# Attention and token-mixing kernel on one core: the last third of x transposed by the DMA, attention in half groups, eager first scores, last store in pieces

## The chip, the cores and the metric

The kernel runs on one core of a Trainium2 chip. The metric is device time in microseconds (us) of one execution. Times below are medians of the fast executions of a kernel; executions of one kernel here lie within 0.2 to 1.4% of each other (kernel before: 223.94 to 224.87). A ratio is the mean time of one kernel's fast runs over that of the other's in the same rounds, so it isn't quite the ratio of the medians that are quoted. A profile covers the span from the first to the last instruction of one execution, some 2 us less than its time; what is counted in a trace is counted in that execution alone.

TensorE is the matrix engine, VectorE and ScalarE the two elementwise engines, GpSimd casts inputs here, and SyncE issues nearly all DMAs. In the profile they are PE, DVE, ACT, POOL and SP; PEld is the weight load of TensorE.

## The reference, cut to what matters

```python
# 8 batches, 16 query heads, 4 key/value heads, 384 positions, head size 64
scores = (1/sqrt(64)) * q @ k.T            # per head
attn   = exp(scores - max) / sum
x      = attn @ v                          # -> 8 x 384 x 1024
wq, wk = x @ w_q, x @ w_k                  # 1024 -> 64
W_tok  = (1/sqrt(64)) * wq @ wk.T          # 384 x 384 per batch
out    = relu(W_tok @ x) @ w_out           # 1024 x 1024
```

The product `x @ [w_q w_k]` needs x with its 1024 features on the partitions, so each batch's x (three thirds of 128 positions) has to be transposed. In the kernel this product is `wqk`; it needs all three thirds, and everything after it for that batch (`wk_tr`, `mix_c`, `mix_m`, `po`) needs its result.

## The kernel before

The order of instructions isn't written out; a small scheduler inside the kernel keeps a clock for TensorE (`clk["pe"]`), estimates when each operand will be there (`ready`), and always emits the best candidate. Each engine gets its list in that order; how strictly TensorE keeps to it shows below, where it stands idle for 4.37 us in front of one instruction with others behind it in the list. The estimates are guesses made when the kernel is built.

```python
    def x_tr_dma(b, c):                                   # third c of batch b, by the DMA
        ...
        nc.sync.dma_start_transpose(out=xTs[b][:, :, c, :], in_=xn[:, c, :])
        ready["T", b, c] = when(("X", b, c, 0), ("X", b, c, 1)) + 4500     # the guess: 4.5 us

    def x_tr(b, c):                                       # the same by TensorE and VectorE
        ...
        for dc in range(DC):
            nc.tensor.transpose(out=ps[:, dc, :], in_=xn[:, c, dc * P:(dc + 1) * P], identity=ident)
        nc.vector.tensor_copy(out=xTs[b][:, :, c, :], in_=ps)

    def attend(b, g):                                     # one group: two halves, a PSUM bank each
        ...
        if b > 0 and c < C - 1 and kp == KP - 1:
            x_tr_dma(b, c)                                # thirds 0 and 1 of batches 1 to 7

    def wqk(b):                                           # needs xT of all three thirds
        ...
        for dc in range(DC):
            nc.tensor.matmul(out=ps, lhsT=wqk_sb[:, dc, :],
                             rhs=xT[:, dc].rearrange("d c p -> d (c p)"),
                             start=(dc == 0), stop=(dc == DC - 1))

    def after_s(b, s):                                    # SyncE's work, tied to the score steps
        n = b + 1
        ...
        if s == 0:
            load(n)                                       # 2.36 MB: keys, queries in two halves, values
        elif s == 5:
            cast(n)                                       # GpSimd, to bf16
            start_tr(n)
        elif s in (9, 11, 13, 15):
            tr_dma(n, (s - 9) // 2)                       # keys, then queries in thirds, transposed by the DMA
```

The loads, the transposes and the stores all go out on SyncE's one queue, in the order in which the scheduler emits them.

The softmax here doesn't subtract the row's maximum and nothing guards it: scores larger than these inputs give would overflow.

## Time and profile before

| | kernel before |
|---|---|
| time, median | 223.95 us (first three runs), 224.35 with a fourth |
| TensorE busy | 92% of 221.7 us |
| ScalarE, VectorE busy | 64%, 65% |
| DMA engines busy | over 90% in most slices up to 160 us |
| waits of TensorE after 45 us | none worth counting |

The prediction below shows the lines. Three more are needed for the comparison: the granted clock of TensorE in 40 slices (9 is 90% or more), the chain of work that ended last, and the group of `wqk` (its columns: line, engine, operation, operands, count, busy us and mean ns, then the idle time just before and what ended it).

```profile
PEclk9999999999999999999999999999999999999999
...
PE 87%; ACT 4%; DVE 4%; issue 2%; DMA 1%; ACTq 0%
...
L328 PE MATMUL bank<-xT,wqk_sb 128*128 128x384 bf16 x64 | 11.8, 327 | 0.0
```

The clock has no dent, the chain is TensorE nearly throughout, and `wqk` never waited: 0.0 us of idle time before its 64 matmuls.

### The profile page before, as it was taken

Reading aid. Unit: us, or ns where it says so; the run is one execution under the profiler, and the core shown is the slowest. Engines: PE = TensorE matmul, PEld = TensorE weight load, DVE = VectorE, ACT = ScalarE, POOL = GpSimd, SP = SyncE. Lnnn points to the kernel's source line nnn. Section 1 sums busy time; section 2 is a strip of 40 time slices with the busy share of each in tenths; the row PEclk is TensorE's granted clock in tenths of the full one; section 3 lists DMA queues with packets and bytes.
Section 4 is the critical chain, followed back from the end, with each engine's and each line's share of the span. In section 5 each row is a group of like instructions: output and inputs, shape, how many; then the busy total and the mean of one; then the engine's idle time right before and its main releaser. Section 6 shows DMA issues by size and latency. Waiting matters only on the chain.

```text
span 221.7 us, 5331 instructions
## 1 busy us (share of the span) xinstructions
PE 204.7 (92%) x2164; PEld 106.5 (48%) x2164; DVE 144.1 (65%) x363; ACT 140.9 (64%) x146; POOL 52.3 (24%) x97
## 2 busy tenths in 40 slices
PE   1686899799999999999999999999999998999992
PEld 0264575446454645454546454644554553434440
DVE  2363776946786678768866687665876578475341
ACT  3588988978877887788788868787778730000000
POOL 1378757304400440027004400260000000000000
PEclk9999999999999999999999999999999999999999
DMA  6999999899869978899999997998422420332433
GB/s 166 329 326 263 418 368 290 159 232 353 132 186 237 348 98 220 196 324 242 154 272 348 147 223 194 336 209 163 142 95 52 142 95 3 146 138 95 191 143 143
DMA packets 71400, 46.09 MB, mean 208 GB/s; under 512 B 42704, under 2 KB 67280, under 8 KB 71376
## 3 DMA queue, kind: packets, MB, share of 16 engines
q1 hardware_dynamic: 71376, 45.75, 78.0%
q8 instruction: 17, 0.28, 0.5%
q14 instruction: 7, 0.06, 0.1%
HBM read 23.59 MB, written 12.58 MB: 163 GB/s over the span
## 4 chain that ended last, share of the span: by engine, by line
PE 87%; ACT 4%; DVE 4%; issue 2%; DMA 1%; ACTq 0%
PE bank L405 39%; PE bank L277 16%; PE sc L247 16%; PE bank L328 5%; ACT pt L251 4%; PE bank L359 3%; PE bank L381 2%; PE bank L319 2%; PE bank L212 2%; DMA kraw<-in_k_dram 1%; DVE xnat L286 1%; DVE wT L334 1%; DVE wq L336 0%; PE bank L346 0%; PE bank L196 0%
## 5 line engine op out<-in xcount | busy, mean ns | idle before, releaser
L251 ACT ACTIVATE pt<-sc 128x1024 bf16<-128x1024 f32 x144 | 139.2, 1021 | 34.9 <-PE sc L247 34.8
L405 PE MATMUL bank<-wout_sb,msb 128*128 128x512 bf16 x384 | 94.6, 380 | 0.3 <-DVE msb L386 0.3
L405 PEld LDWEIGHTS <-msb 128*128 128x128 bf16 x384 | 33.9, 97 | 45.9 <-issue 14.5
L247 PE MATMUL sc<-QT,KT 64*128 64x512 bf16 x288 | 46.2, 389 | 5.1 <-ACT pt L251 3.9
L277 PEld LDWEIGHTS <-pt 128*128 128x128 bf16 x1152 | 41.3, 98 | 14.0 <-issue 4.6
L414 DVE COPY osb<-bank 128x512 f32<-128x512 f32 x48 | 33.0, 688 | 21.8 <-PE bank L405 21.6
L277 PE MATMUL bank<-vext,pt 128*128 128x65 bf16 x1152 | 45.4, 194 | 1.4 <-ACT pt L251 1.4
L286 DVE TENSOR_TENSOR xnat<-bank,rcp 128x256 bf16<-128x256 f32 x96 | 40.8, 425 | 3.3
L386 DVE TENSOR_SCALAR msb<-bank 128x384 bf16<-128x384 f32 x64 | 32.3, 550 | 3.9 <-PE bank L381 3.7
L146 POOL CAST qb<-qraw 128x768 bf16<-128x768 f32 x30 | 24.0, 829 | 19.4 <-DMA qraw<-in_q_dram 15.7
L285 DVE RECIPROCAL rcp<-bank 128x4 f32<-128x4 f32 x96 | 17.0, 177 | 17.5 <-PE bank L277 17.1
L247 PEld LDWEIGHTS <-KT 64*128 64x128 bf16 x288 | 12.9, 94 | 25.8 <-issue 21.8
L141 POOL CAST kb<-kraw 128x192 bf16<-128x192 f32 x30 | 9.2, 350 | 65.9 <-DMA kraw<-in_k_dram 65.9
L328 PE MATMUL bank<-xT,wqk_sb 128*128 128x384 bf16 x64 | 11.8, 327 | 0.0
L381 PE MATMUL bank<-wq,Csb 64*128 64x384 bf16 x32 | 10.4, 326 | 0.1
L381 PE MATMUL bank<-wT,Csb 64*128 64x384 bf16 x32 | 10.4, 326 | 0.0
L363 DVE CAST Csb<-bank 128x512 bf16<-128x512 f32 x8 | 5.5, 692 | 7.5 <-PE bank L359 7.5
L334 DVE CAST wT<-bank 128x384 bf16<-128x384 f32 x8 | 4.5, 558 | 7.7 <-PE bank L328 7.7
L320 DVE COPY xT<-bank 128x1024 bf16<-128x1024 bf16 x10 | 6.7, 688 | 3.6 <-PE bank L319 3.6
L586 POOL CAST wout_sb<-wld 128x1024 bf16<-128x1024 f32 x8 | 8.1, 1042 | 3.9 <-DMA wld<-in_moe_w_out_dram 3.9
L328 PEld LDWEIGHTS <-wqk_sb 128*128 128x128 bf16 x64 | 5.7, 98 | 5.6 <-issue 1.9
L154 POOL CAST vext<-vraw 128x384 bf16<-128x384 f32 x16 | 7.8, 510 | 0.0
(30 smaller groups left out, 55.2 us busy)
## 6 DMA issues: line engine op xcount, KB each, us to landing
out_dram<-osb SPq DMA_DIRECT2D x24, 512.0 KB, 2.8
qraw<-in_q_dram SPq DMA_DIRECT2D x15, 768.0 KB, 8.7
wld<-in_moe_w_out_dram SPq DMA_DIRECT2D x4, 1024.0 KB, 8.2
kraw<-in_k_dram SPq DMA_DIRECT2D x7, 384.0 KB, 4.3
vraw<-in_v_dram SPq DMA_DIRECT2D x7, 384.0 KB, 9.2
qraw<-in_q_dram SPq DMA_DIRECT2D x1, 512.0 KB, 6.0
kraw<-in_k_dram SPq DMA_DIRECT2D x2, 192.0 KB, 4.2
vraw<-in_v_dram SPq DMA_DIRECT2D x2, 192.0 KB, 6.8
```

The costliest lines, as they stand in the source:

```text
L141: eng.tensor_copy(out=nats[b][0][:, kp, :, u, :], in_=raws[b][0][:, 2 * kp + u])
L146: eng.tensor_copy(out=nats[b][1][:, :, kp, :, u, :].rearrange("p c i d -> p i c d"), in_=raws[b][2][:, h0:h0 + G])
L247: nc.tensor.matmul(out=ps[:, u, :], lhsT=KT[lo:hi, kp * C + kc, :], rhs=QT[lo:hi, t0:t0 + G, :].rearrange("k i p -> k (i p)"), start=True, ...
L251: nc.scalar.activation(out=pt.rearrange("k u i p -> k u (i p)"), in_=ps, func=AF.Exp, scale=attn_scale)
L277: nc.tensor.matmul(out=outs[u][:, i * DE:i * DE + D + 1], lhsT=tiles[kc][:, u, i, :], rhs=vext[:, 2 * kp + u, kc, :D + 1], start=(kc == 0) ...
L285: nc.vector.reciprocal(out=rcp, in_=avv[:, :, D])
L286: nc.vector.tensor_tensor(out=xout[:, u], in0=avv[:, :, :D], in1=rcp.to_broadcast([P, G, D]), op=ALU.mult)
L328: nc.tensor.matmul(out=ps, lhsT=wqk_sb[:, dc, :], rhs=xT[:, dc].rearrange("d c p -> d (c p)"), start=(dc == 0), stop=(dc == DC - 1))
L381: nc.tensor.matmul(out=bank_ps[i][:, :S], lhsT=Csb[lo:hi, j * P:(j + 1) * P], rhs=w[lo:hi, :], start=True, stop=True)
L386: nc.vector.tensor_scalar_max(out=msb[:, dc, :], in0=bank_ps[i][:, :S], scalar1=0.0)
L405: nc.tensor.matmul(out=ps, lhsT=msbs[b][:, dc, c * P:(c + 1) * P], rhs=wout_sb[:, dc, half * NH:(half + 1) * NH], start=(nd == 0), stop=(n ...
L414: nc.vector.tensor_copy(out=osb[:, half * NH:(half + 1) * NH], in_=ps)
```

## The change

Its intent: take 48 transposes off TensorE, the engine that sets the time; let attention start when one PSUM bank is free rather than two; feed ScalarE without gaps in batch 0; hold the column-tiled product (`mix_c`) back when a score burst is near; and let the last store start earlier. Cut to its core:

```diff
+    EAGER = 0
+    DMA_TR = 5500
@@ guesses of the scheduler for a DMA transpose
-                ready["K", b, kp] = clk["pe"] + 4500
+                ready["K", b, kp] = clk["pe"] + DMA_TR
@@ attend: one half u per call, one bank
-    def attend(b, g):
+    def attend(b, g, u):
 ...
-        if b > 0 and c < C - 1 and kp == KP - 1:
+        if x_by_dma(b, c) and kp == KP - 1:
             x_tr_dma(b, c)
+
+    def x_by_dma(b, c):
+        return b > 0 and (c < C - 1 or b < B - 1)
@@ po: the last store
+            if last:
+                (nc.sync if n0 % NH == 0 else nc.scalar).dma_start(out=dst[:, n0:n1], in_=osb[:, n0:n1])
@@ chain_open
-            if b == 0 or c == C - 1:
+            if not x_by_dma(b, c):
                 todo.append((..., lambda c=c: x_tr(b, c), 1))
-        todo.append((lambda: when(("N", b)), lambda: mix_c(b), 1))
+        todo.append((lambda: when(("N", b)), lambda: mix_c(b), 1, "tiled"))
@@ step
-            row = todo[0][2] == 2
-            if row and pair is not None and pair < now + 1200:
+            if todo[0][-1] == "tiled" and pair is not None and pair < now + 1200:
                 prio = 6
-            cands.append((s0 + 30, 7, go_s))
+            cands.append((s0, 0, go_s) if state["S"][0] <= EAGER else (s0 + 30, 7, go_s))
```

More of the change, by code (lines that the diff above doesn't have):

```diff
@@ L185, in tr_dma @@
             for kp in range(KP):
-                ready["Q", b, kp, c] = clk["pe"] + 4500
+                ready["Q", b, kp, c] = clk["pe"] + DMA_TR
     def tr_k(b, kp0, kp1):
@@ L253, in scores @@
         pts[b, s] = pt
-        done = on("act", 1020, pe(225, "row"))
+        done = on("act", 1020, pe(225 if b else 430, "row"))
         clk["act"] = done - 60 - 100
@@ L257, in scores @@
         ready["P", b, s] = done
-    def attend(b, g):
+    def attend(b, g, u):
         kp, c = groups(b)[g]
         vext = vexts[b % 3]
-        if g == 0:
+        if g == 0 and u == 0:
             xnats[b] = x_p.tile([P, C, Hq, D], BF16, name="xnat", bufs=3)
-        xnat = xnats[b]
-        tiles = [pts.pop((b, C * g + kc)) for kc in range(C)]
-        h0 = 2 * kp * G
-        xout = xnat[:, c, h0:h0 + 2 * G, :].rearrange("p (u i) d -> p u i d", u=2)
-        if NWIDE:
-            _, at = wide()
-            outs = [wide_ps[at][:, u, :] for u in range(2)]
-        else:
-            two = [bank(u)[1] for u in range(2)]
-            outs = [bank_ps[i] for i in two]
-        for u in range(2):
-            for i in range(G):
-                for kc in range(C):
-                    nc.tensor.matmul(out=outs[u][:, i * DE:i * DE + D + 1],
-                                     lhsT=tiles[kc][:, u, i, :],
-                                     rhs=vext[:, 2 * kp + u, kc, :D + 1],
-                                     start=(kc == 0), stop=(kc == C - 1))
-            if NWIDE:
-                continue
-            avv = outs[u][:, :G * DE].rearrange("p (i e) -> p i e", i=G)
-            rcp = small_p.tile([P, G], F32, name="rcp", bufs=4)
-            nc.vector.reciprocal(out=rcp, in_=avv[:, :, D])
-            nc.vector.tensor_tensor(out=xout[:, u], in0=avv[:, :, :D],
-                                    in1=rcp.to_broadcast([P, G, D]), op=ALU.mult)
-            done = bank_free[two[u]] = on("dve", 665, pe(370))
-        if NWIDE:
-            avv = wide_ps[at][:, :, :G * DE].rearrange("p u (i e) -> p u i e", i=G)
-            rcp = small_p.tile([P, 2, G], F32, name="rcp")
-            nc.vector.reciprocal(out=rcp, in_=avv[:, :, :, D])
-            nc.vector.tensor_tensor(out=xout, in0=avv[:, :, :, :D],
-                                    in1=rcp.to_broadcast([P, 2, G, D]), op=ALU.mult)
-            done = wide_free[at] = on("dve", 935, pe(750))
-        ready["X", b, c, kp] = done
-        if b > 0 and c < C - 1 and kp == KP - 1:
@@ new lines, in attend @@
+        tiles = [pts[b, C * g + kc] for kc in range(C)]
+        at = bank()[1]
+        ps = bank_ps[at]
+        for i in range(G):
+            for kc in range(C):
+                nc.tensor.matmul(out=ps[:, i * DE:i * DE + D + 1], lhsT=tiles[kc][:, u, i, :],
+                                 rhs=vext[:, 2 * kp + u, kc, :D + 1],
+                                 start=(kc == 0), stop=(kc == C - 1))
+        avv = ps[:, :G * DE].rearrange("p (i e) -> p i e", i=G)
+        rcp = small_p.tile([P, G], F32, name="rcp", bufs=4)
@@ new lines, in attend @@
+        nc.vector.reciprocal(out=rcp, in_=avv[:, :, D])
+        h0 = (2 * kp + u) * G
+        nc.vector.tensor_tensor(out=xnats[b][:, c, h0:h0 + G, :], in0=avv[:, :, :D],
+                                in1=rcp.to_broadcast([P, G, D]), op=ALU.mult)
+        bank_free[at] = on("dve", 665, pe(370 if b else 630))
+        if u == 0:
+            return
+        for kc in range(C):
+            pts.pop((b, C * g + kc))
+        ready["X", b, c, kp] = bank_free[at]
+        if x_by_dma(b, c) and kp == KP - 1:
@@ L310, in x_tr_dma @@
         nc.sync.dma_start_transpose(out=xTs[b][:, :, c, :], in_=xn[:, c, :])
-        ready["T", b, c] = when(("X", b, c, 0), ("X", b, c, 1)) + 4500
+        ready["T", b, c] = when(("X", b, c, 0), ("X", b, c, 1)) + DMA_TR
     def x_tr(b, c):
@@ L413, in po @@
         osb = osbs[b, c]
-        nc.vector.tensor_copy(out=osb[:, half * NH:(half + 1) * NH], in_=ps)
+        dst = out[b].rearrange("(p c) n -> c p n", c=C)[c]
+        last = b == B - 1 and c == C - 1
+        for n0 in range(half * NH, (half + 1) * NH, NH // 2 if last and half else NH):
+            n1 = n0 + (NH // 2 if last and half else NH)
+            nc.vector.tensor_copy(out=osb[:, n0:n1], in_=ps[:, n0 - half * NH:n1 - half * NH])
+            if last:
+                (nc.sync if n0 % NH == 0 else nc.scalar).dma_start(out=dst[:, n0:n1], in_=osb[:, n0:n1])
         bank_free[i] = on("dve", 690, end)
-        if half == 1:
-            nc.sync.dma_start(out=out[b].rearrange("(p c) n -> c p n", c=C)[c], in_=osb)
-    state = {"S": (0, 0), "A": (0, 0)}
+        if half == 1 and not last:
+            nc.sync.dma_start(out=dst, in_=osb)
+    state = {"S": (0, 0), "A": (0, 0, 0)}
     prep = []
@@ L454, in cand_a @@
     def cand_a():
-        b, g = state["A"]
+        b, g, u = state["A"]
         if b == B:
             return None
-        return max(when(*[("P", b, C * g + kc) for kc in range(C)]), ready["V", b],
-                   wide()[0] if NWIDE else bank(1)[0])
+        return max(when(*[("P", b, C * g + kc) for kc in range(C)]), ready["V", b], bank()[0])
     def go_a():
-        b, g = state["A"]
-        attend(b, g)
-        if g + 1 == C * KP:
+        b, g, u = state["A"]
+        attend(b, g, u)
+        if u == 0:
+            state["A"] = (b, g, 1)
+        elif g + 1 == C * KP:
             chain_open(b)
-            state["A"] = (b + 1, 0)
+            state["A"] = (b + 1, 0, 0)
         else:
-            state["A"] = (b, g + 1)
+            state["A"] = (b, g + 1, 0)
     def chain_open(b):
@@ L476, in chain_open @@
         todo.append((lambda: when(("W", b)), lambda: wk_tr(b), 1))
-        todo.append((lambda: when(("N", b)), lambda: mix_c(b), 1))
+        todo.append((lambda: when(("N", b)), lambda: mix_c(b), 1, "tiled"))
         for j in range(DC // 2):
-            todo.append((lambda: when(("C", b), ("W2", b)), lambda j=j: mix_m(b, j), 2))
+            todo.append((lambda: when(("C", b), ("W2", b)), lambda j=j: mix_m(b, j), 2, "tiled"))
         chains[b] = todo
@@ L484, in cand_chain @@
     def cand_chain(b):
-        at, _, width = chains[b][0]
-        if chains.get(b - 2) or (width == 2 and any(job[0] <= b - 2 for job in bulk)):
+        at, _, width = chains[b][0][:3]
+        if chains.get(b - 2) or (len(chains[b]) == DC // 2 and any(job[0] <= b - 2 for job in bulk)):
             return INF
@@ L542, in step @@
                 todo = chains[b]
-                if todo and todo[0][2] == 2 and cand_chain(b) <= clk["pe"] + 20:
+                if todo and todo[0][-1] == "tiled" and cand_chain(b) <= clk["pe"] + 20:
                     todo.pop(0)[1]()
@@ L604 @@
         pass
-    assert state["A"] == (B, 0) and not bulk and not prep
+    assert state["A"] == (B, 0, 0) and not bulk and not prep
 _INS = ['q', 'k', 'v', 'moe_w_q', 'moe_w_k', 'moe_w_out']
```

## The prediction

> **What bounds the kernel now.** I read the page's busy shares and slices first, then the groups, then the waits of TensorE, and last the timeline of the SyncE queue with the landing times of single DMAs.
>
> ```profile
> PE 204.7 (92%) x2164; PEld 106.5 (48%) x2164; DVE 144.1 (65%) x363; ACT 140.9 (64%) x146; POOL 52.3 (24%) x97
> ...
> PE   1686899799999999999999999999999998999992
> ...
> DMA  6999999899869978899999997998422420332433
> ```
>
> TensorE is full from slice 8 (some 45 us) to slice 39; before that it waits for inputs and for ScalarE's exponentials. What is easily missed is the last line: the DMA engines are nearly as full as TensorE, up to about 160 us.
>
> ```profile
> PE sc L247 <- ACT pt L251: 3.9, 6, 1.0
> PE bank L277 <- ACT pt L251: 1.4, 4, 0.4
> PE sc L247 <- DVE QT L222: 1.0, 2, 0.5
> ```
>
> These are the longest of TensorE's waits after the one for the first keys (4.2 us), and every one falls in the first 44 us. So in the middle the time is the sum of what TensorE is given, and any new wait of TensorE there is paid in full, since nothing is idle that could be used up later.
>
> ```profile
> 71.83 0.62 PE L319 MATMUL bank<-ident,xnat 128*128 128x128 bf16 x8
> 72.29 0.81 PE L405 MATMUL bank<-wout_sb,msb 128*128 128x512 bf16 x3
> 72.94 0.91 PE L277 MATMUL bank<-vext,pt 128*128 128x65 bf16 x24
> 73.78 0.61 PE L247 MATMUL sc<-QT,KT 64*128 64x512 bf16 x4
> 74.31 1.47 PE L328 MATMUL bank<-xT,wqk_sb 128*128 128x384 bf16 x8
> ```
>
> This stretch of TensorE's timeline gives the prices, start to start: eight transposes 0.46 us (71.83 to 72.29), three output matmuls 0.65 (0.216 each), 24 attention matmuls 0.75 plus about 0.1 for the change to the 64-row form, four score matmuls 0.43 plus 0.1 for the change back, eight of the x-by-weights product (L328) 1.31. L328 is the instruction to watch: it needs all three thirds of the transposed x.
>
> ```profile
> 67.74 0.57 SPq L117 DMA_DIRECT2D kraw<-in_k_dram  x1
> 68.36 1.17 SPq L117 DMA_DIRECT2D qraw<-in_q_dram  x2
> 69.56 2.00 SPq L117 DMA_DIRECT2D vraw<-in_v_dram  x1
> 71.76 1.26 SPq L417 DMA_DIRECT2D out_dram<-osb  x1
> 78.85 1.23 SPq L310 DMA_TRANSPOSE xT<-xnat  x1
> ```
>
> That is the SyncE queue around one batch load, and these are the sizes and landing times of the store at 71.76 and, for comparison, of one in the quiet end (188.31):
>
> ```profile
> out_dram<-osb SPq DMA_DIRECT2D x1, 512.0 KB, 8.3
> ...
> out_dram<-osb SPq DMA_DIRECT2D x1, 512.0 KB, 2.6
> ```
>
> The same store takes 8.3 us instead of 2.6 because it was issued right behind 2.3 MB of loads. It landed at 80.0, which is 12.3 us after the load's first issue. Two more stores behind loads did so after 12.6 us (45.72 to 58.3; 111.86 to 124.5).
>
> **What the Trainium skill says.** "DMA: Bandwidth & Descriptors", section "Queues, rings and completion order": SyncE owns one row of rings, one on each of the 16 DMA engines, and each engine consumes descriptors in ring order. The trace agrees: everything is on one queue, and the store above waited out the load. The same page, "Latency and other measured facts", gives a DMA transpose 261 GB/s; here it is slower: the transpose issued at 174.22 moves 256 KB at about 210 GB/s, some 1.25 us, and lands 3.1 us after issue when nothing is ahead. "TensorEngine Tiling (Array Packing)", "Key Properties": changing the tiling mode drains the engine; the 0.1 us at each change agrees. "TensorE: Matmul & The Clock Gate", Part 1: an idle window of about 3.4 us halves the clock. Here the last matmul ends at 217.4 and the granted clock reads 1.00 up to 220.7 and 0.50 after it, so 3.3 us.
>
> **The change, part by part.** I compared the order of instructions of both kernels engine by engine.
>
> *Transposes.* For batches 1 to 6 the last third goes to the DMA: 48 transposes leave TensorE, 6 x 0.46 = 2.8 us, and six copies of 0.69 us leave VectorE, which isn't the bound. The second part, the column-tiled product held back until a score burst is near, was meant to save mode changes. In the order as built it doesn't: between blocks of 128-row, 64-row and 64-column form I count 171 changes before and 183 after. Past the first output matmul it is 134 against 144: ten more. From 45.0 to 217.4 us (172.4 us) TensorE ran 156.7 us worth of blocks at the prices above, so a change costs (172.4 - 156.7)/134 = 0.117 us; ten more cost 1.2 us. Net of this part: 2.8 - 1.2 = **1.6 us saved**.
>
> *Half groups and eager scores.* Attention now takes one PSUM bank at a time and is cut in 12s between output matmuls: same form, no cost. In batch 0 a score pair is issued as soon as a PSUM slot is free. ScalarE starts at 7.18 us and had some 3.7 us of gaps over the first 18 exponentials, which end at 27.45. Laying the new order out by hand, at 0.915 us per exponential, I get 25.1. Following it to the first output matmul (both kernels have done exactly the same 72 score and 264 attention matmuls by then) gives 42.2 against 44.94: **2.7 us saved**, if the inputs of batch 2 are there. Their first query transpose is issued at 40.13, held by casts of data that land at 38.4, and lands at 43.3: just in time.
>
> *Last store.* Its last piece is 128 KB instead of 512 KB. Of the 2.6 us, about 1.3 is movement (512 KB at some 400 GB/s), of which a quarter stays: about **0.8 us saved** after the small extra copy.
>
> *What is added.* Six DMA transposes, about 1.25 us of all 16 engines each, on engines over 90% busy. The cost is not their size but their place. In the new SyncE order each third transpose of batch b, for b = 1 to 5, stands **directly behind the load of batch b+2**. By the 12.3 to 12.6 us above it lands about 12.5 us after that load's first issue. Before, the two transposes of a batch were issued at least 9 us after the load in front of them began, and the third was TensorE's own. TensorE's new order places L328 some 7 us after the last attention matmul of its batch. I add the blocks in the new order, with "load" the first issue of the load (an output store before it in the queue has to be issued first, about 1.35 us after its last matmul: evacuation 0.9, issue 0.45):
> - Batch 1: SyncE reaches the load at 45.4, tied to the landings of the startup; the transpose lands at about 57.7. TensorE, 2.7 us early, arrives at 45.3 + 7.3 = 52.6. Wait 5.1.
> - Batch 2: last attention matmul 0.2 us after the load, plus 7.4: arrives at 7.6, data at 12.5. Wait 4.9.
> - Batch 3: 2.5 after, plus 6.8: 9.3. Wait 3.2.
> - Batch 4: the queue is held by two transposes, load 3.75 us after group 3; attention ends at 7.15, plus 6.85: 14.0 against 16.3. Wait 2.3.
> - Batch 5: 1.3 after, plus 7.0: 8.3. Wait 4.2.
> - Batch 6: there is no further load; 3.2 us to land, hidden. Wait 0.
>
> Sum **19.7 us**. TensorE takes its instructions in order, so output matmuls standing behind L328 can't fill the hole. Three of these waits are longer than 3.4 us and may let the clock drop; one window at half clock loses about 1.7 us, and since a wait of 4 to 5 us contains a whole window only about half the time, I add 1.3 us.
>
> Total: -1.6 - 2.7 - 0.8 + 19.7 + 1.3 = +15.9 on 223.95, or about 239.8; I say **239.5 us**.
>
> **Rivals.** *Hidden transposes.* The schedule allows 5.5 us from x to its transpose, and if transposes landed in 3.2 us as all isolated ones do, all would be hidden: 223.95 - 5.1 = 219 us, faster by 2.3%. For it: the change is plainly meant so, and 14 of 14 transposes before landed in 3.1 to 5.0 us. Against it: none of those stood behind a load, and the three stores that did took 6.5 to 8.3 us.
>
> *Half of the wait.* If the relation of load and attention slips by some 2 us per batch (the load reached earlier in the queue, or VectorE holding the attention's output back), the waits sum to about 10 us: 229 to 231 us, slower by 3%. For it: my sums leave out small waits, and the three short waits are within 2 us of half. Against: the store in front of the load ties it to TensorE's own order.
>
> *DMA as the bound.* A batch moves 2.3 MB of loads (7 us), three stores (3.9), and now seven transposes (about 8.5): 19.4 of some 22 us, before gaps. With the gaps that transposes leave while they are being issued it could reach the period, and every transpose would be late: 245 to 250 us. For it: shares over 0.9 in all the middle. Against: a TensorE that waits lengthens the period and so relieves the DMA.
>
> **Range and chances.** The low end of 230 is the second rival, the high end of 248 the third. Faster needs the FIFO reading to be wrong: 0.06. Within 2% needs the waits to be a quarter of what I add up: 0.07. Slower: 0.87.
>
> **What would show it.** Right: in the changed profile TensorE's (or its weight load's) waits list L328 on the DMA of xT, five times, 2 to 5 us each, the first ending near 57.7 us; third transposes of batches 1 to 5 land 7 us or more after issue, the others in 3 to 5; the sixth isn't waited for; the first output matmul starts near 42 us; there are 2116 matmuls; the clock dips after the longest waits. Wrong: L328 without a wait, or transposes landing in 3 to 4 us although right behind a load; then the time is near 219 us.

## The result

| | before | changed |
|---|---|---|
| time, median | 224.35 us | 246.63 us (246.13 to 247.88, 4 runs) |
| ratio of fast runs | 1 | 1.100 (95%: 1.0945 to 1.1055) |
| profiled span | 221.7 us | 244.3 us |
| TensorE's waits for transposed x | 0 | 19.6 us, five times |
| mean granted clock | 0.998 | 0.963 |

The profiled execution took 246.13 us; the other three had a mean clock of 0.958, so they lost a little more to it than the trace below shows. Of the page of the changed kernel, these lines answer to those shown of before: busy time, TensorE, its granted clock and the DMA in 40 slices, the chain of work that ended last, by engine and by line, and the group of `wqk` (now L321):

```profile
PE 208.4 (85%) x2088; PEld 104.9 (43%) x2116; DVE 140.8 (58%) x358; ACT 140.5 (58%) x146; POOL 52.2 (21%) x97
...
PE   1798998984999479984999599975999999999994
...
PEclk9999999998899979998999979997999999999999
DMA  7999999999097981999359959799264253222344
...
PE 71%; DMA 17%; ACT 5%; DVE 3%; issue 3%; DVEq 0%; ACTq 0%
PE bank L398 31%; DMA xT<-xnat 15%; PE sc L249 14%; PE bank L272 11%; PE bank L321 6%; ACT pt L253 5%; PE bank L374 3%; PE bank L352 3%; PE bank L214 2%; DMA kraw<-in_k_dram 1%; DVE xnat L279 1%; PE bank L312 1%; PE bank L339 1%; DVE Csb L356 1%; DVE osb L411 0%
...
L321 PE MATMUL bank<-xT,wqk_sb 128*128 128x384 bf16 x64 | 15.2, 393 | 19.8 <-DMA xT<-xnat 19.6
```

TensorE has five holes where it had none (the lowest digits of its row from the tenth slice on: 4, 4, 4, 5 and 5; the 4 in the last slice is the end of the work), the clock row has a dent at each, and the DMA has gone from 1% to 17% of the chain. Of these, 15% are the transposes of x, in front of one instruction: L321, with 19.6 us of idle time before it. The mean of L321 also rose from 327 to 393 ns: that is the clock. (The count 2088 is 28 short of the 2116 weight loads; some matmul records are missing from the trace.)

One of the five, batch 2, in the SyncE queue (start, duration, issue) with the time to landing of this transpose, and then in TensorE's timeline (in brackets: idle before, and what ended it):

```profile
74.42 0.43 SPq L119 DMA_DIRECT2D kraw<-in_k_dram  x1
74.90 1.98 SPq L119 DMA_DIRECT2D qraw<-in_q_dram  x2
76.93 2.72 SPq L119 DMA_DIRECT2D vraw<-in_v_dram  x1
79.75 3.46 SPq L303 DMA_TRANSPOSE xT<-xnat  x1
```

```profile
xT<-xnat SPq DMA_TRANSPOSE x1, 6.6
```

```profile
86.43 2.74 PE L321 MATMUL bank<-xT,wqk_sb 128*128 128x384 bf16 x8 [4.37 <-DMA xT<-xnat]
```

The transpose is issued right behind the load, lands at 86.39 (79.75 + 6.63), 12.0 us after the load's first issue, and TensorE starts 0.04 us later. The eight matmuls then take 2.74 us where the prediction's stretch of the kernel before shows 1.47. The view by stretches says why: busy time of the engines over the idle 4.3 us, over the 3.4 us that follow, and over the next 3.4 us; the number before the DMA share is the granted clock.

```profile
82.10:86.40 4.30, 0.00 (x0) 0.00 (x0) 0.46 (x2) 1.78 (x2) 3.56 (x5) 1.00 1.20 255
86.40:89.80 3.40, 3.17 (x9) 1.35 (x10) 0.57 (x2) 0.00 (x0) 0.54 (x2) 0.50 1.17 287
89.80:93.20 3.40, 3.29 (x43) 1.73 (x45) 1.82 (x6) 2.32 (x3) 0.00 (x0) 1.00 0.00 0
```

TensorE ran at half clock for one stretch of 3.4 us (its 9 matmuls and the 43 of the next stretch are of different sizes; the eight of L321, 2.74 us against 1.47, are the fair comparison). The trace has five such stretches inside the work, each 3.41 us long, starting at 59.1, 86.4, 113.7, 141.0 and 168.3 us. At half clock 3.41 us of TensorE does 1.7 us worth of work, so five cost 5 x 1.7 = 8.5 us.

So 19.6 us of waits and 8.5 us of slow clock, 28.1 together, stand against a rise of 22.3 us (246.63 - 224.35). The difference, some 6 us, would be what the change saves. The experiments test each of these three numbers.

### The profile page after: what moved, and what is told of

Read it like the earlier page. It is cut to its first block, busy times and chain, and to the rows that moved or that the text cites. A ratio compares the mean times of both kernels' runs of the same rounds, so it can differ in the third digit from the quotient of the medians.

```text
span 244.3 us, 5219 instructions
## 1 busy us (share of the span) xinstructions
PE 208.4 (85%) x2088; PEld 104.9 (43%) x2116; DVE 140.8 (58%) x358; ACT 140.5 (58%) x146; POOL 52.2 (21%) x97
## 4 chain that ended last, share of the span: by engine, by line
PE 71%; DMA 17%; ACT 5%; DVE 3%; issue 3%; DVEq 0%; ACTq 0%
PE bank L398 31%; DMA xT<-xnat 15%; PE sc L249 14%; PE bank L272 11%; PE bank L321 6%; ACT pt L253 5%; PE bank L374 3%; PE bank L352 3%; PE bank L214 2%; DMA kraw<-in_k_dram 1%; DVE xnat L279 1%; PE bank L312 1%; PE bank L339 1%; DVE Csb L356 1%; DVE osb L411 0%
## 5 line engine op out<-in xcount | busy, mean ns | idle before, releaser
L398 PE MATMUL bank<-wout_sb,msb 128*128 128x512 bf16 x356 | 93.0, 385 | 2.0 <-issue 1.2
L249 PE MATMUL sc<-QT,KT 64*128 64x512 bf16 x288 | 49.0, 406 | 4.4 <-ACT pt L253 2.6
L272 PEld LDWEIGHTS <-pt 128*128 128x128 bf16 x1152 | 42.1, 98 | 16.8 <-issue 9.0
L272 PE MATMUL bank<-vext,pt 128*128 128x65 bf16 x1152 | 46.8, 195 | 0.6 <-ACT pt L253 0.4
L411 DVE COPY osb<-bank 128x512 f32<-128x512 f32 (+1 forms) x49 | 33.1, 677 | 23.0 <-PE bank L398 21.9
L321 PE MATMUL bank<-xT,wqk_sb 128*128 128x384 bf16 x64 | 15.2, 393 | 19.8 <-DMA xT<-xnat 19.6
L148 POOL CAST qb<-qraw 128x768 bf16<-128x768 f32 x30 | 24.0, 827 | 16.4 <-DMA qraw<-in_q_dram 14.1
L249 PEld LDWEIGHTS <-KT 64*128 64x128 bf16 x288 | 12.6, 95 | 28.1 <-issue 24.0
L321 PEld LDWEIGHTS <-wqk_sb 128*128 128x128 bf16 x64 | 6.7, 110 | 25.7 <-issue 13.9
L352 PE MATMUL bank<-xnat,wkN 128*64 128x512 bf16 x48 | 6.7, 387 | 0.0
```

Of the source, the lines that this page charges most:

```text
L148: eng.tensor_copy(out=nats[b][1][:, :, kp, :, u, :].rearrange("p c i d -> p i c d"), in_=raws[b][2][:, h0:h0 + G])
L249: nc.tensor.matmul(out=ps[:, u, :], lhsT=KT[lo:hi, kp * C + kc, :], rhs=QT[lo:hi, t0:t0 + G, :].rearrange("k i p -> k (i p)"), start=True, ...
L272: nc.tensor.matmul(out=ps[:, i * DE:i * DE + D + 1], lhsT=tiles[kc][:, u, i, :], rhs=vext[:, 2 * kp + u, kc, :D + 1], start=(kc == 0), sto ...
L321: nc.tensor.matmul(out=ps, lhsT=wqk_sb[:, dc, :], rhs=xT[:, dc].rearrange("d c p -> d (c p)"), start=(dc == 0), stop=(dc == DC - 1))
L352: nc.tensor.matmul(out=ps[half * Dh:(half + 1) * Dh, :], lhsT=wkN[:, c, :], rhs=xn[:, c, half * NH:(half + 1) * NH], start=(c == 0), stop= ...
L398: nc.tensor.matmul(out=ps, lhsT=msbs[b][:, dc, c * P:(c + 1) * P], rhs=wout_sb[:, dc, half * NH:(half + 1) * NH], start=(nd == 0), stop=(n ...
```

## The experiments

**My theory**: the third transposes land late only because they stand in one queue behind a load, TensorE waits for them, and the waits make its clock drop. **Rivals**: the DMA engines are full, so that the extra transposes cost by their bytes wherever they stand; or half groups, eager scores or more mode changes cost the time. The kernel before ran in every job's rounds, at 223.87 to 224.24 us. Every run gave correct results.

### The third by TensorE again

```diff
-        return b > 0 and (c < C - 1 or b < B - 1)
+        return b > 0 and c < C - 1
```

> The changed kernel with one part undone: the last third of x goes through TensorE again in batches 1 to 6; half groups, eager scores, the held-back product and the split last store stay. My theory (third transposes landing late behind the batch loads, plus the clock dips that these waits cause) expects no wait of the x-by-weights product on a transpose, no clock dip, and 222 to 223.5 us (224.35 less 1.5 of startup and 0.8 of tail, plus 0.9 for eight more mode changes). A rival, that half groups, eager scores or mode changes cost the time, expects it to stay above 235.

Measured: 220.56 us, ratio 0.985 (0.983 to 0.988). There is no wait for a transpose and no clock dip in its trace. The second rival falls: with half groups, eager scores and eight more mode changes than before (179 against 171), the kernel is *faster* than before. I had expected 222 to 223.5, so these parts gain 3.5 us instead of about 1.4.

### The load behind the transpose

```diff
-        if s == 0:
+        if s == 2:
             load(n)
```

> The changed kernel with only the place of the batch load moved: it is issued at the third score step of a batch instead of the first, so it stands behind the third transpose in the DMA queue and not ahead of it. TensorE's order of instructions is the same, and so are the bytes. My theory expects the third transposes to land 3 to 4 us after issue, no waits for them, no dips, and 218 to 221 us. The rival that the DMA engines have become the bound (seven transposes a batch are too many bytes) expects the same waits as before, moved at most, and over 238. The risk in mine is that the load is now some 3 us later, which could delay the casts and query transposes of the batch after next.

Measured: 218.17 us, ratio 0.974 (0.972 to 0.977). It beats both kernels. TensorE's list is, line for line, that of the changed kernel (buffer numbers aside), and so are the bytes; in SyncE's list the load and the third transpose change places, once in each of batches 1 to 5, and nothing else differs. The same batch 2 as above, SyncE, landing and TensorE:

```profile
70.46 1.51 SPq L303 DMA_TRANSPOSE xT<-xnat  x1
72.02 0.57 SPq L119 DMA_DIRECT2D kraw<-in_k_dram  x1
```

```profile
xT<-xnat SPq DMA_TRANSPOSE x1, 4.1
```

```profile
74.90 0.92 PE L272 MATMUL bank<-vext,pt 128*128 128x65 bf16 x24
75.75 0.61 PE L249 MATMUL sc<-QT,KT 64*128 64x512 bf16 x4
76.28 1.47 PE L321 MATMUL bank<-xT,wqk_sb 128*128 128x384 bf16 x8
```

The transpose lands at 74.5, TensorE reaches L321 at 76.28 without a pause, and the eight matmuls take 1.47 us again. The third transposes of batches 1 to 5 took 3.2, 4.1, 4.6, 4.8 and 3.2 us to land, two of them clearly more than the 3 to 4 expected. It is now the first third of the following batch that stands behind the load: in batches 2 to 6 it landed 6.6 to 8.8 us after issue, and TensorE waited for none of them. The first rival, the bytes, falls with this run. From 218.17 to 246.63 are 28.5 us (27.7 between the two profiled executions); the waits and the dips, counted in the trace, were 28.1.

### Filler for the clock

```diff
         ps = bank_ps[i][:, :S]
+        if 0 < b < 6:
+            for _ in range(18):
+                nc.tensor.matmul(out=ps, lhsT=ident, rhs=wout_sb[:, 0, :S], start=True, stop=True)
```

> The changed kernel with work added that nobody reads: 18 matmuls of 384 columns (18 x 0.162 = 2.9 us) just ahead of each waiting x-by-weights product of batches 1 to 5, into the bank that the product then overwrites. They run while TensorE would stand idle for the transpose. My theory says that the five clock dips (3.41 us each at half clock, some 1.7 us lost each, 8.5 in all) come from these idle stretches: with the filler the waits shorten to 0 to 1.6 us, the dips go, and the time falls by 6 to 9 us to 237.5 to 241, although 14.6 us of TensorE work is added. If the dips don't come from the idle stretches or cost nothing, it stays at 246 to 248.

Measured: 240.50 us, ratio 1.074 (1.071 to 1.078), 6.1 us less than the changed kernel. Adding 90 useless matmuls made it faster. In the trace, the first line the filler and the second the product:

```profile
80.30 3.10 PE L322 MATMUL bank<-wout_sb,ident 128*128 128x384 bf16 x18
84.65 1.47 PE L324 MATMUL bank<-xT,wqk_sb 128*128 128x384 bf16 x8 [1.25 <-DMA xT<-xnat]
```

The wait is down to 1.25 us and the product at full speed. Four of the five dips are gone; in the profiled execution the fifth stayed, after a wait of 2.73 us, longer than the 1.6 expected. Four dips are worth 6.8 us; the filler and what is left of the waits (14.6 + 5.8 = 20.4 us) take 0.8 us more than the waits did (19.6). 6.8 - 0.8 = 6.0, and 6.1 was measured between the medians, 5.3 between the profiled executions (246.13 and 240.82). The other three executions with filler have mean clocks of 0.998 to 1.000, which leaves no room for the fifth dip, so the sum is good to a microsecond or two. The dips come from the idle time, and their price is about right.

### Transposes that nobody reads

The kernel before, with the six extra transposes sent into memory that is free by then:

```diff
+        if 0 < b < B - 1 and c == C - 1 and kp == KP - 1:
+            xn = xnats[b].rearrange("p c h d -> p c (h d)")
+            spare = wld.bitcast(BF16)[:, b, :Dm].rearrange("p (a s) -> p a s", a=DC)
+            nc.sync.dma_start_transpose(out=spare, in_=xn[:, c, :])
```

> The kernel before, with the six extra DMA transposes issued where the change issues them, into memory that nobody reads; TensorE still makes the third itself, in the same order. It measures what the extra transposes cost as traffic, without anybody waiting for them. My theory expects 223.5 to 226 us, the same as before, with these transposes landing 6.5 to 8.5 us after issue in batches 1 to 5 and 3 to 4.5 us in batch 6. The rival that traffic is the bound expects over 229.

Measured: 224.10 us, ratio 1.001 (0.999 to 1.004). No cost of the traffic is visible (the interval allows 0.8 us at most). The extra transpose of batch 2, issued at 71.49 behind the load:

```profile
wld<-xnat SPq DMA_TRANSPOSE x1, 8.3
```

In batches 1 to 5 they landed 8.4, 8.3, 6.7, 7.6 and 8.0 us after issue; in batch 6, with no load ahead, in 3.1.

### The product later in TensorE's order

```diff
+    X3_TR = 12000
-        ready["T", b, c] = when(("X", b, c, 0), ("X", b, c, 1)) + DMA_TR
+        ready["T", b, c] = when(("X", b, c, 0), ("X", b, c, 1)) + (X3_TR if c == C - 1 and b < B - 2 else DMA_TR)
```

> The changed kernel with the place of the load and of every transpose kept, but the kernel's own schedule told that the third transposes of batches 1 to 5 take 12 us instead of 5.5. TensorE then gets about six groups of other work ahead of the x-by-weights product. My theory: the transposes land as late as ever (6.5 to 8.5 us after issue), but nobody stands still for them, no dips, 218 to 222 us. The rival that the lateness itself holds something else up (bytes, stores, later transposes) expects over 230.

Measured: 222.39 us, ratio 0.993 (0.990 to 0.995). The third transposes of batches 1 to 5 landed 7.5 to 8.4 us after issue, as late as ever, without a wait for them and without a dip. So it isn't lateness that makes the waits and the dips, but lateness with an instruction waiting at the head of TensorE's list. The time is just over the range, 4 us more than with the load moved. This version's order differs in many places, and I haven't found which of them costs the 4 us; that some of it comes from the late transposes isn't excluded here, though the unread ones cost nothing visible.

### The third alone

The kernel before with nothing but

```diff
-        if b > 0 and c < C - 1 and kp == KP - 1:
+        if b > 0 and (c < C - 1 or b < B - 1) and kp == KP - 1:
-            if b == 0 or c == C - 1:
+            if b == 0 or (c == C - 1 and b == B - 1):
```

> The kernel before with nothing but the third transposes of batches 1 to 6 given to the DMA. By my theory this part alone carries the loss: some 4 us of wait in each of five batches and five dips, 243 to 254 us. If half groups or eager scores are needed for the loss, it stays under 232.

Measured: 256.98 us (2 runs), ratio 1.147 (1.143 to 1.150), above my range. This part alone carries the loss, and more: the waits are 4.5, 5.8, 5.7, 5.0 and 5.0 us, and four of the five dips last 6.8 us, twice 3.41. The old guess of 4.5 us, which lets the product stand earlier, is the likely reason; no run tests it.

### Dose: half of the load, then a sixth, behind the transpose

```diff
+            four = [lambda: ld(kraw, k, 0, 4), lambda: ld(qraw, q, 0, half),
+                    lambda: ld(qraw, q, half, Hq), lambda: ld(vraw, v, 0, 4)]
+            for go in four[:2] if b > 2 else four:    # 3 in the smaller dose
+                go()
+            rest[b] = four[2:] if b > 2 else []
@@ after_s
+        elif s == 2:
+            for go in rest[n]:
+                go()
```

> Dose: the changed kernel with half of each later load (second half of the queries and the values, 1.18 MB of 2.36) issued behind the third transpose, the other half left ahead; TensorE's order is unchanged. At the 340 GB/s that the loads reach, 1.18 MB is 3.5 us, so the waits of 4.3, 4.4, 3.9, 2.8 and 4.2 us should shrink to about 0.8, 0.9, 0.4, 0 and 0.7, the dips should go, and the time should be 219.5 to 223.5 us. If it isn't the bytes ahead but merely standing near a load that matters, the waits stay above 3 us and the time above 240.

> Smaller dose: only the values (0.39 MB, 1.15 us at 340 GB/s) behind the third transpose. The waits should each shrink by about 1.15 us, to 3.2, 3.2, 2.8, 1.7 and 3.1 us, three to five dips should stay, and the time should be 237 to 241.5 us. The other reading (nearness, not bytes) expects 246 again.

Measured: 223.51 us (ratio 0.996) with half behind, 236.48 us (ratio 1.055, 1.048 to 1.061) with a sixth. Batch 2's product, half first, then the sixth:

```profile
78.18 1.48 PE L322 MATMUL bank<-xT,wqk_sb 128*128 128x384 bf16 x8 [1.48 <-DMA xT<-xnat]
```

```profile
83.05 1.88 PE L322 MATMUL bank<-xT,wqk_sb 128*128 128x384 bf16 x8 [3.75 <-DMA xT<-xnat]
```

| bytes ahead | third lands, us after the load's first issue | waits of batches 1 to 5, us | sum | dips | time: median, profiled |
|---|---|---|---|---|---|
| 2.36 MB (changed kernel) | 12.0 to 12.6 | 4.3, 4.4, 3.9, 2.8, 4.2 | 19.6 | 5 | 246.63, 246.13 |
| 1.97 MB | 10.1 to 11.3 | 2.3, 3.8, 2.3, 1.9, 3.0 | 13.3 | 4 | 236.48, 237.38 |
| 1.18 MB | 8.0 to 10.0 | 0.3, 1.5, 1.3, 0, 1.7 | 4.7 | 0 | 223.51, 223.63 |
| 0 | | 0 | 0 | 0 | 218.17, 218.41 |

The landing and the wait follow the bytes that stand ahead, not mere nearness. The sums expected were 14.0 and 2.8 us. The smaller dose came out 0.5 us below its range, the half at the top of its own. Between the profiled executions the time falls by 19.0 us from the second to the last row; waits and dips (13.3 + 4 x 1.7) account for 20.1. From the third row it is 5.2 against 4.7. The dips vary between executions: with a sixth behind, the mean clock was 0.968 in the profiled one and 0.978 to 0.984 in the others; with half behind, 1.000 and 0.992 to 0.997.

### What the other parts are worth

All on top of the version with the load moved:

```diff
-    EAGER = 0                                  # no eager scores
+    EAGER = -1
```

> The version with the load behind the third transpose (218.2 us), with the eager score pairs of batch 0 taken out again. It prices the startup part. By my working eager scores brought the first output matmul 2.7 us forward; the traces so far show 1.1 to 2.4 us. So the time should rise by 1 to 2.7 us, to 219.2 to 221 us. If the startup gain is lost later (in a wait for the casts or transposes of batch 2), it stays within 0.5 us of 218.2.

```diff
-        last = b == B - 1 and c == C - 1       # last store whole
+        last = False
```

> The same version (218.2 us) with the last store whole again, one DMA of 512 KB. It prices the tail part. From the last output matmul to the end of the span the kernel before took 4.3 us and the changed one 3.5, so the time should rise by 0.8 us, to about 219.0. If the end is set by something else, it stays at 218.2.

```diff
-        attend(b, g, u)                        # whole groups
-        if u == 0:
-            state["A"] = (b, g, 1)
-        elif g + 1 == C * KP:
+        attend(b, g, 0)
+        attend(b, g, 1)
+        if g + 1 == C * KP:
```

> The version with the load behind the third transpose (218.2 us), with attention in whole groups again (two banks taken together, 24 matmuls without anything between). It prices the half groups. The other parts add up to 1.8 (eager), 0.74 (store) and 2.4 (transposes off TensorE) of the 5.9 us that this version saves over the kernel before, so if half groups are the rest the time should rise by about 0.9 us to 219.1. This order has 175 mode changes against 183; if a mode change costs 0.117 us everywhere, that alone would lower it by 0.9 us, to 217.3.

> The version with the load behind the third transpose once more, on the same chip and in the same rounds as the whole groups, so that the two can be compared within 0.3%: 218.2 us, 2.6% under the kernel before.

Measured: 219.98 us without eager scores (1.8 more) and 218.91 with a whole last store (0.7 more). The store's ratio, 0.978 (0.975 to 0.981), overlaps that of the version it is compared with, so its 0.7 us rests on the traces: from the last output matmul to the end of the span 4.4 us with the whole store, 3.5 without. With whole groups 218.31 us were measured, against 217.80 for the same version in the same rounds. These last two ratios, 0.975 (0.972 to 0.978) and 0.973 (0.971 to 0.975), overlap: half groups are worth 0.5 us by the medians, and the runs don't show that it is more than nothing. The fifth part needed no run: built (not run) with the old rule for the product that is held back, the version with the load moved has exactly the same lists on every engine. That part of the diff moved nothing.

## Why the prediction was right, point by point

**The time** (239.5, range 230 to 248, slower at 0.87) was right: 246.63, inside the range near its high end. In part that is luck: the prediction's own sum gives 239.8, and the high end of 248 was put there for the third rival (245 to 250), whose mechanism the runs refute. The number alone couldn't have told the two apart.

**The step from queue to wait** held. Third transposes behind loads landed 6.6 to 8.3 us after issue and 12.0 to 12.6 us after the load's first issue, as the prediction's 12.3 to 12.6 had it, the sixth in 3.1; L321 waited for a transpose in exactly the five batches named and not in the sixth. The first landed at 58.25 (57.7 foretold). The waits, foretold as 5.1, 4.9, 3.2, 2.3 and 4.2 us, were 4.3, 4.4, 3.9, 2.8 and 4.2: sum 19.7 foretold, 19.6 measured, single ones off by up to 0.8. That the sum agrees so closely is partly luck.

**The term that was mis-sized is the clock**: "only about half the time, I add 1.3 us". It was 8.5 us, five dips instead of less than one. There was a slip in the sum, too: three waits, each with a dip half the time, at 1.7 us are 2.6 us and not 1.3. The failing step was the condition: I let a dip happen only if a whole window of 3.4 us was idle. The runs show dips after waits of 2.3 us, so every wait of the changed kernel was long enough. In each trace the clock changes only at times that lie a whole number of 3.41 us apart. In the five windows of that length just before its dips, the changed kernel's TensorE was idle for 2.73, 3.41, 3.05, 2.10 and 2.76 us: only the second was idle throughout. With 8.5 in place of 1.3 the working gives 247.0 (239.8 + 7.2).

**The savings** were 5.1 foretold, 5.9 measured (224.03 to 218.17, with the load moved), but differently made up. With them the account closes: 19.6 + 8.5 - 5.9 = 22.2, against the rise of 22.3. Eager scores: 2.7 foretold, 1.8 measured. Store: 0.8 and 0.7. Transposes off TensorE: 1.6 net foretold; the version with the load moved is 2.4 us faster than the one with the third by TensorE, close to the gross 2.8 (the two differ in the load's place as well). The deduction for mode changes didn't show: eight or more of them were added without a visible loss, and the order with eight fewer (whole groups, 175 against 183) wasn't faster, though it differs in more than that. The 0.117 us had put all small losses between blocks down to mode changes. The first output matmul came at 43.46 instead of 42, in part because the clock's first release, which falls anywhere between 12.0 and 16.4 us in these traces, was late (14.7): with the same eager half groups it comes at 42.5 where the release is at 12.0 and at 43.8 where it is at 16.1.

**The rivals** were rightly set aside. The first, hidden transposes at 219 us, is what the kernel does once the load stands behind (218.2): the change was sound but for one place in a queue. The second, half of the wait, didn't come: 19.6 us and not 10. The third, the DMA as the bound, fell with the unread transposes (224.10).

## What to carry to other kernels

The waits for a DMA were set here by the bytes issued ahead of it on the same queue, not by its own size: before moving work from a full engine to the DMA, read the issue order and put the small transfer that someone waits for ahead of the large one that nobody needs yet. When a kernel's own schedule rests on a guess of a transfer's time, compare the guess (5.5 us here) with landing times measured behind a load (6.6 to 8.3 after issue, and the issue itself was late). And a wait on TensorE costs more than its length: here each one of 2.3 us or more was followed by 3.4 us or more at half clock.

## What the Trainium skill lacked or had wrong

- "TensorE: Matmul & The Clock Gate", Part 1 and "Why this matters for your kernels", says that the clock drops after at least one idle window of about 3.4 us and advises against idle gaps over about 3 us. Here waits of 2.3 us were enough (with a sixth of the load behind: dips after 2.31 and 2.34 us), while waits of 1.9 us and less caused none. The half-clock stretches last 3.41 us or twice that, which agrees with the page's window; in the changed kernel they start 27.3 us apart, eight windows. But a window needn't be idle throughout: 1.92 us of idle time inside one was followed by half clock, 1.86 us wasn't (both with a sixth of the load behind), nor was 1.94 us at the end of the run with the product later.
- "DMA: Bandwidth & Descriptors", "Latency and other measured facts", gives 261 GB/s for a DMA transpose with a non-contiguous middle dimension and 350 to 400 for a contiguous one; here 256 KB took about 1.25 us of movement, 210 GB/s, and 3.1 us from issue to landing on an idle queue.
- The same page, "Queues, rings and completion order", was right: in-order rings. I found no page that says what this does to the issuing queue: in the changed kernel a transpose takes SyncE 1.23 us to issue when nothing is ahead and 3.4 to 3.6 us right behind a load, and the next DMA goes out only after it (in batch 2 the store, at 83.31).
- "TensorEngine Tiling (Array Packing)", "Key Properties", says that a mode change drains the engine and gives no cost. About 0.1 us is visible at each boundary, but eight changes more or fewer didn't show in the time of a whole kernel.
